# Attention and gated MLP on one core: which engine copies kv wo, the first attention product in four matmuls, and a new hand-searched order

## The chip, the cores and the metric

One core of one Trainium2 chip. Its engines are TensorE (PE), VectorE (DVE), ScalarE (ACT), GpSimd (POOL) and SyncE (SP, which here only issues DMA transfers). Each engine works through its own queue in order and waits on semaphores. The metric is the device time of one execution in microseconds; the figure before is the median of three runs.

## The reference

A block of two parts over x of 2048 x 512 (bfloat16), cut to what is computed:

```
ln(t)  = (t - mean) / sqrt(var + 1e-5)
phi(t) = where(t > 0, t + 1, exp(t)) + 1e-6

q, k, v = ln(x) @ wqkv            # 32 heads of 16
kv  = phi(k)^T v                  # per head, 16 x 16
z   = sum over rows of phi(k)
o   = phi(q) kv / (phi(q) z + 1e-6)
h   = x + o @ wo

zz  = gelu(ln(h) @ w_in)          # 1792 wide
z1, z2 = zz[:, :896], ln(zz[:, 896:])
g   = w_sp @ z2 + b_sp            # w_sp is 2048 x 2048
out = h + (z1 * g) @ w_out
```

## The kernel before

The rows are 16 tiles of 128. Everything stays on the chip; x, the weights and the transposed w_sp are loaded, the output is stored.

**Stages.** Row tiles are normalised and transposed (the first four on PE, the rest by DMA transposes, line 673). k products (lines 745 and 756) are followed by phi: ACT's exponential (714) and relu (720), DVE's minimum (716) and sum (722) or, without relu, maximum (725). In place of k and v, the sum over rows of ln(x)^T phi(k) is built up in four PSUM banks (766). After the last tile it is copied (799, 802), multiplied by wv (811), masked to the heads' blocks (820) and multiplied by wo (827): that gives `mw`, kv wo, four blocks of 128 x 512 in PSUM. Blocks 0 and 2 are copied to SBUF by ACT (834), blocks 1 and 3 by DVE (837). q products (858) and phi run between all this in groups of four tiles; a group's denominators are made by a small matmul (871), ACT takes ln and exp (875, 878), SP spreads the result over the partitions (884), and DVE multiplies phi(q) by it (890).

**The attention product** (903) takes, for each row tile, four matmuls of 512 columns that read the four blocks of `mw` in turn; DVE adds x (916), takes the statistics, POOL the power -0.5 (608, 610), DVE normalises, SP transposes. Then come the right half of w_in (959) with gelu on ACT (966 with sums, 974 without), the left half (1013, gelu 1018), the mix with w_sp (1052; DVE 1058, 1060), and the output product (1072, 1076).

**The order.** `build` records each operation with its engine, a cost, what it reads and writes, and a due time `want`. `Program.schedule` (line 151) walks forward in planned time and puts the operations of every engine in a fixed order: of the operations whose predecessors are already placed, each engine takes the one with the lowest planned start plus half its due time. `waits` (line 264) then writes the semaphore waits. On the chip each engine follows its list in order. The due times are the list `WANT` (line 359), one number for each recorded operation, times `UNIT`. `fillers` (line 1097) puts useless matmuls (575) into PE's planned gaps before the first product of line 766, so that PE's clock stays up; eight more run at the start.

**The SP queue.** SP issues all loads (538), the transposes of x and h tiles (673), the spreads (884), and the 64 transposes of w_sp (1032): `wsp0.0` to `wsp0.15` fill the first quarter of the mix's right side, `wsp1.x` the second, and so on. wq, wv, wo, win and wout are one load each (lines 666 to 670).

Of the kernel before, what the change touches and what calls it, by code (L numbers as in the profile page):

```python
# [10 lines left out]
P = 128  # L11
# [81 lines left out]
class Program:  # L93
# [264 lines left out]
UNIT = 0.1  # L358
WANT = [
# [40 lines left out]
def build(nc, A_x, A_wqkv, A_wo, B_w_in, B_w_sp, B_b_sp, B_w_out, out):  # L400
    _, S, D = A_x.shape
    F = B_w_in.shape[1]
    FH = F // 2
# [21 lines left out]
    UNIT_RES = set()  # L425

# [52 lines left out]
    eps = small([4], FP32)  # L479
    mhalf = small([TPG], FP32)  # L480
# [65 lines left out]
    for p in range(1, NP):  # L546
        load("sp", f"x{2 * p}", x[2 * p:2 * p + 2, :],
             x_dram[2 * p * P:(2 * p + 2) * P, :].rearrange("(n p) d -> p n d", p=P), 2 * P * D * 2, -28 + p)

# [89 lines left out]
    def T1(n):  # L639
        return 5.2 + 1.85 * n  # L640

    rs1, cT = {}, {}
    for grp in LN1:
        rs = small([len(grp)], FP32)
        nm = small([len(grp)], FP32) if any(n in ACT_NORM1 for n in grp) else None
        for n in grp:
            stats(x[n, :], Row(st_x, n), T1(n) - 4, f"st{n}")
            aggr(Row(st_x, n), 6, T1(n) - 4, f"ag{n}")
        lo, hi = grp[0], grp[-1] + 1
        for n in grp:  # L650
            if n in LATE:
                d, m = xc[n].all(), st_x[n, 6:7]
                cT[n] = Tile(XC)
                op("dve", dve_f(512), lambda e, n=n, d=d, m=m: e.tensor_scalar(d.ap(), x[n, :].ap(), m.ap(), None,
                                                                              op0=ALU.subtract),
                   r=[x[n, :], m], w=[d, cT[n]()], want=T1(n) - 3, name=f"xc{n}")
        rstd_act(st_x[lo:hi, 7], rs.all(), T1(lo) - 2.5, f"rs{lo}")
        if nm is not None:
            minus_mean(st_x[lo:hi, 6], rs.all(), nm.all(), T1(lo) - 2.5, f"nm{lo}")
        for i, n in enumerate(grp):  # L660
            rs1[n] = rs[i:i + 1]
            if n in ACT_NORM1:
                normalise_act(xn[n, :], x[n, :], nm[i:i + 1], rs[i:i + 1], T1(n) - 2, f"xn{n}")
            else:
                normalise(xn[n, :], x[n, :], st_x[n, 6:7], rs[i:i + 1], T1(n) - 2 + 4 * (n in LATE), f"xn{n}")
# [3 lines left out]
    load("sp", "win", win.all(), B_w_in.rearrange("(c p) f -> p c f", p=P), D * F * 2, 30.2)  # L669
    load("sp", "wout", wout.all(), B_w_out.rearrange("(c p) f -> p c f", p=P), FH * D * 2, 30.3)  # L670
# [133 lines left out]
    for b in range(2):  # L804
# [26 lines left out]
        for i in range(2):  # L831
            d = mw[2 * b + i, :]
            if i == 0:
                op("act", act_c(512), lambda e, t=t, d=d: e.activation(d.ap(), t(bank(0)).ap(), ACT.Copy), r=[t()], w=[d],
                   want=T0 + 3.5 + b, name=f"mwc{2 * b}")
            else:
                op("dve", dve_c(512), lambda e, t=t, d=d: e.tensor_copy(d.ap(), t(bank(1)).ap()), r=[t()], w=[d],  # L837
                   want=T0 + 3.5 + b, name=f"mwc{2 * b + 1}")
# [54 lines left out]
    hn_t, hn_op = {}, {}  # L893
    for p in range(NP):
        t = Tile(PS, 2)
        for ti in range(2):
# [4 lines left out]
            def mm(e, t=t, ti=ti, l=l, n=n, unit=unit):  # L901
# [5 lines left out]
                return i  # L907
            op("pe", pe_c(*[512] * (4 + unit)), mm, r=[l, mw.all()] + ([x[n, :], ident.all()] if unit else []), w=[t()],
# [12 lines left out]
    for grp in LN2:  # L921
# [8 lines left out]
        for i, n in enumerate(grp):  # L930
            t = hn_t[n] = Tile(HN)
            if n in ACT_NORM2:
                hn_op[n] = normalise_act(t(), x[n, :], nm[i:i + 1], rs[i:i + 1], w0 + 1 + 0.1 * i, f"hn{n}")
            else:
                hn_op[n] = normalise(t(), x[n, :], st_h[n, 6:7], rs[i:i + 1], w0 + 1 + 0.1 * i, f"hn{n}")

# [3 lines left out]
    for p in range(NP):  # L940
# [11 lines left out]
        for n in (2 * p, 2 * p + 1):  # L952
# [12 lines left out]
            if n in ACT_Z:  # L965
                op("act", (act_c(FH)[0] + 0.1, act_c(FH)[1] + 0.1), lambda e, t=t, d=d, n=n: e.activation(  # L966
# [6 lines left out]
            else:  # L973
                op("act", act_c(FH), lambda e, t=t, d=d: e.activation(d.ap(), t(flat).ap()[:, 0:FH], ACT.Gelu_apprx_tanh),
# [52 lines left out]


# [149 lines left out]
```

## Time and profile before

| | |
|---|---|
| runs (us) | 243.06, 242.39, 242.1; median 242.39 |
| profiled execution: device time, span | 242.13 us, 240.4 us |
| TensorE clock granted | 1.0 of full speed, throughout |
| POOL busy | 14.2 us (6%) |
| DMA | 24.18 MB, mean 101 GB/s |
| attention products (903) in the chain that ended last | 5.8% of the span |
| mix products (1052) in that chain | 40.0% of the span |

A row of an instruction view gives start, length, engine, line, operation, tiles and count; brackets give the engine's idle time just before and who ended it. The ends of matmuls are modelled: a matmul's row is longer than its distance to the next one. The chain of waits gives start, length, and the work that held the end up in that stretch. In tables by stretch the columns are the stretch, its length, the busy time and instruction count of PE, PE's weight loads, DVE, ACT and POOL, the granted clock, the DMA engines' mean busy share, and GB/s.

### The profile page before, as it was taken

Reading aid. Unit: us, or ns where it says so; the run is one execution under the profiler, and the core shown is the slowest. Engines: PE = TensorE matmul, PEld = TensorE weight load, DVE = VectorE, ACT = ScalarE, POOL = GpSimd, SP = SyncE. Lnnn points to the kernel's source line nnn. Section 1 sums busy time; section 2 is a strip of 40 time slices with the busy share of each in tenths; the row PEclk is TensorE's granted clock in tenths of the full one; section 3 lists DMA queues with packets and bytes.
Section 4 is the critical chain, followed back from the end, with each engine's and each line's share of the span. In section 5 each row is a group of like instructions: output and inputs, shape, how many; then the busy total and the mean of one; then the engine's idle time right before and its main releaser. Section 6 shows DMA issues by size and latency. Waiting matters only on the chain.

```text
span 240.4 us, 3056 instructions
## 1 busy us (share of the span) xinstructions
PE 235.1 (98%) x1177; PEld 108.6 (45%) x1199; DVE 127.4 (53%) x270; ACT 83.4 (35%) x131; POOL 14.2 (6%) x33
## 2 busy tenths in 40 slices
PE   8999999999999999999999999999999999999996
PEld 2444445444444544444444444444444444444443
DVE  5999756299999983227212333324333433332443
ACT  4898965566065799994211100000000000000000
POOL 3000000001202160213000000000000000000000
PEclk9999999999999999999999999999999999999999
DMA  6986789632632545445444544452200001000022
GB/s 195 292 206 81 206 199 313 225 102 95 173 84 56 88 100 107 91 99 100 99 97 104 83 99 108 93 107 66 87 0 0 25 22 44 0 3 0 0 87 87
DMA packets 61805, 24.18 MB, mean 101 GB/s; under 512 B 52064, under 2 KB 61152, under 8 KB 61792
## 3 DMA queue, kind: packets, MB, share of 16 engines
q1 hardware_dynamic: 61648, 23.97, 41.2%
q8 instruction: 9, 0.15, 0.3%
q10 hardware_dynamic: 144, 0.03, 0.1%
q14 instruction: 4, 0.03, 0.1%
HBM read 7.47 MB, written 2.10 MB: 40 GB/s over the span
## 4 chain that ended last, share of the span: by engine, by line
PE 94%; DVE 3%; ACT 1%; issue 1%
PE ps L1052 40%; PE ps L1072 10%; PE ps L959 10%; PE ps L1013 10%; PE ps L903 6%; PE ps L766 6%; PE ps L756 5%; PE ps L858 4%; PE ps L575 2%; DVE hT L802 1%; DVE k_xn_z L837 1%; DVE xT_pq_z L890 0%; PE ps L684 0%; DVE xT_pq_z L725 0%; PE ps L778 0%
## 5 line engine op out<-in xcount | busy, mean ns | idle before, releaser
L1052 PE MATMUL ps<-wsp,k_xn_z 128*128 128x512 bf16 x328 | 73.6, 379 | 0.4
L1058 DVE TENSOR_TENSOR e<-ps,e 128x512 bf16<-128x512 f32 x28 | 19.4, 691 | 69.2 <-PE ps L1052 69.2
L1052 PEld LDWEIGHTS ps<-wsp,k_xn_z 128*128 128x128 bf16 x336 | 32.9, 98 | 39.7
L1013 PE MATMUL ps<-hT,win 128*128 128x512 bf16 x110 | 26.0, 379 | 0.1
L959 PE MATMUL ps<-win,hT 128*128 128x384 bf16 (+1 forms) x126 | 25.3, 352 | 0.1
L1072 PE MATMUL ps<-wout,xT_pq_z 128*128 128x512 bf16 (+2 forms) x125 | 25.1, 355 | 0.1
L1052 PE MATMUL ps<-wqkv_wsp,k_xn_z 128*128 128x512 bf16 x110 | 24.2, 379 | 0.1
L1018 ACT ACTIVATE xT_pq_z<-ps 128x1024 bf16<-128x1024 f32 x14 | 14.1, 1021 | 25.5 <-PE ps L1013 25.5
L587 DVE BATCH_NORM_STATS2 small<-xh 128x6 f32<-128x512 bf16 x32 | 21.0, 679 | 3.0 <-DMA xh<-in_A_x_dram 2.9
L959 PEld LDWEIGHTS ps<-win,hT 128*128 128x128 bf16 x128 | 12.5, 98 | 12.4
L1072 PEld LDWEIGHTS ps<-wout,xT_pq_z 128*128 128x128 bf16 x126 | 11.8, 98 | 12.7
L1052 PEld LDWEIGHTS ps<-wqkv_wsp,k_xn_z 128*128 128x128 bf16 x112 | 11.0, 98 | 13.2
L1013 PEld LDWEIGHTS ps<-hT,win 128*128 128x128 bf16 x112 | 11.0, 98 | 12.6
L1076 DVE TENSOR_TENSOR e<-ps,xh 128x512 bf16<-128x512 f32 (+2 forms) x18 | 11.3, 632 | 9.7 <-PE ps L1072 9.2
L714 ACT ACTIVATE e<-ps 128x1024 bf16<-128x1024 f32 (+1 forms) x16 | 15.4, 970 | 2.0 <-PE ps L756 1.1
L766 PE MATMUL ps<-k_xn_z 128*128 128x512 bf16 x63 | 15.2, 379 | 0.2 <-issue 0.2
L858 PE MATMUL ps<-xT_pq_z,wqkv_wsp 128*128 128x512 bf16 x61 | 15.0, 379 | 0.1
L903 PE MATMUL ps<-k_xn_z,xT_pq_z 128*128 128x512 bf16 x62 | 14.0, 379 | 0.6 <-DVE k_xn_z L837 0.4
L966 ACT ACTIVATE k_xn_z<-ps 128x896 bf16<-128x896 f32 x12 | 10.9, 909 | 9.2 <-PE ps L959 9.2
L756 PE MATMUL ps<-wqkv_wsp,xT_pq_z 128*128 128x512 bf16 x55 | 13.2, 379 | 0.3 <-ACT xT_pq_z L699 0.2
L1060 DVE TENSOR_TENSOR xT_pq_z<-xT_pq_z,e 128x512 bf16<-128x512 bf16 x28 | 11.9, 425 | 2.2 <-ACT xT_pq_z L1018 1.3
L970 ACT ACTIVATE e<-k_xn_z 128x896 bf16<-128x896 bf16 x12 | 11.4, 949 | 0.3
(75 smaller groups left out, 168.6 us busy)
## 6 DMA issues: line engine op xcount, KB each, us to landing
wsp<-e SPq DMA_DIRECT2D x16, 128.0 KB
out_dram<-e SPq DMA_DIRECT2D x15, 128.0 KB, 1.7
xh<-in_A_x_dram SPq DMA_DIRECT2D x7, 256.0 KB, 3.8
win<-in_B_w_in_dram SPq DMA_DIRECT2D x1, 1792.0 KB, 7.5
wqkv_wsp<-in_A_wqkv_dram SPq DMA_DIRECT2D x3, 512.0 KB, 5.7
wout<-in_B_w_out_dram SPq DMA_DIRECT2D x1, 896.0 KB, 5.3
wsp<-in_B_w_sp_dram SPq DMA_TRANSPOSE x48, 2.7
wqkv_wsp<-in_A_wo_dram SPq DMA_DIRECT2D x1, 512.0 KB, 5.0
```

What stands on the lines that cost most here:

```text
L587: op("dve", (0.577, 0.69), lambda e: e.bn_stats(row[0:6].ap(), src.ap()), r=[src], w=[row[0:6]], want=want, name=name)
L714: first = op("act", act_c(n, ptr=len(pt)), lambda e: e.activation(e_(ev).ap(), src(t), ACT.Exp, scale=sc), r=[t()] + pt, w=[e_()], want=wa ...
L756: i = e.matmul(t(bank(ti)).ap(), lhsT=lhs.ap()[:, c, :], rhs=rhs.ap()[:, c, :], start=(c == 0), stop=(c == KD - 1))
L766: i = e.matmul(HT(bank(j)).ap(), lhsT=xn[n, j * P:(j + 1) * P].ap(), rhs=pk[n, :].ap(), start=(n == 0), stop=(n == NT - 1))
L858: k = e.matmul(t(bank(i)).ap(), lhsT=lhs.ap()[:, c, :], rhs=rhs.ap()[:, c, :], start=(c == 0), stop=(c == KD - 1))
L903: i = e.matmul(t(bank(ti)).ap(), lhsT=l.ap()[:, c, :], rhs=mw[c, :].ap(), start=(c == 0), stop=(c == KD - 1 and not unit))
L959: k = e.matmul(t(bank(i)).ap()[:, 0:b - a], lhsT=l.ap()[:, c, :], rhs=win[c, a:b].ap(), start=(c == 0), stop=(c == KD - 1))
L1013: k = e.matmul(t(bank(i)).ap(), lhsT=l.ap()[:, c, :], rhs=r_.ap()[:, c, :], start=(c == 0), stop=(c == KD - 1))
L1018: op("act", act_c(1024), lambda e: e.activation(d.ap(), t(None if same else flat).ap(), ACT.Gelu_apprx_tanh), r=[t()], w=[d], want=want + ...
L1052: k = e.matmul(t(bank(0)).ap(), lhsT=l.ap()[:, s - a, :], rhs=r_.ap()[:, s - a, :], start=(s == 0), stop=(s == NT - 1))
L1058: op("dve", dve_c(512), lambda e: e.tensor_tensor(gb().ap(), t(bank(0)).ap(), bsp().ap()[:, tg * GW:(tg + 1) * GW], ALU.add), r=[t(), bsp( ...
L1072: k = e.matmul(t(bank(0)).ap()[:, 0:r_.ap().shape[-1]], lhsT=l.ap()[:, fc, :], rhs=r_.ap()[:, fc, :], start=(fc == 0), stop=(fc == KF - 1))
```

## The change

- ACT copies blocks 0, 2 and 3 of `mw`; DVE copies block 1 alone.
- The attention product of row tile 2 (`FIRST_O = 2`) is recorded as four operations of one matmul each, on blocks 2, 0, 1, 3 in this order, each reading its own block.
- The load of win has to come after the normalisation of row tile 15 (`xn_op`); the load of wout is recorded after the left-half products and has to come after the gelu of row tile 8 (`g2_op`).
- `UNIT` is 0.02 in place of 0.1, and all of `WANT` is new. From the output products on, and for the mix products of the last two quarters, the due times are the same as before in microseconds.

```
-UNIT = 0.1
+UNIT = 0.02
 WANT = [
...
+    FIRST_O = 2
...
-    load("sp", "win", win.all(), B_w_in.rearrange("(c p) f -> p c f", p=P), D * F * 2, 30.2)
-    load("sp", "wout", wout.all(), B_w_out.rearrange("(c p) f -> p c f", p=P), FH * D * 2, 30.3)
+    load("sp", "win", win.all(), B_w_in.rearrange("(c p) f -> p c f", p=P), D * F * 2, 30.2, after=[xn_op[NT - 1]])
...
-            if i == 0:
-                op("act", act_c(512), lambda e, t=t, d=d: e.activation(d.ap(), t(bank(0)).ap(), ACT.Copy), r=[t()], w=[d],
-                   want=T0 + 3.5 + b, name=f"mwc{2 * b}")
+            if i == 0 or b == 1:
+                op("act", act_c(512), lambda e, t=t, d=d, i=i: e.activation(d.ap(), t(bank(i)).ap(), ACT.Copy), r=[t()],
+                   w=[d], want=T0 + 3.5 + b, name=f"mwc{2 * b + i}")
             else:
                 op("dve", dve_c(512), lambda e, t=t, d=d: e.tensor_copy(d.ap(), t(bank(1)).ap()), r=[t()], w=[d],
                    want=T0 + 3.5 + b, name=f"mwc{2 * b + 1}")
...
+            if n == FIRST_O:
+                for k, c in enumerate((2, 0, 1, 3)):
+                    op("pe", pe_c(512), lambda e, t=t, ti=ti, l=l, k=k, c=c: e.matmul(
+                        t(bank(ti)).ap(), lhsT=l.ap()[:, c, :], rhs=mw[c, :].ap(), start=(k == 0), stop=(k == KD - 1)),
+                       r=[l, mw[c, :]], w=[t()], want=TO(p) + 0.01 * k, name=f"o{n}.{c}" if k else f"o{n}")
+                continue
...
+    load("sp", "wout", wout.all(), B_w_out.rearrange("(c p) f -> p c f", p=P), FH * D * 2, 300.0, after=[g2_op[8]])
```

The due times (in us) that the prediction speaks of:

| load or transpose | before | after |
|---|---|---|
| wv | 39.6 | 19.4 |
| wo | 39.0 | 58.0 |
| win | 31.8 | 32.1 |
| wout | 24.8 | 88.06 |
| wsp1.0 | 109.7 | 108.24 |
| wsp0.12 | 111.0 | 109.54 |

More of the change, by code (lines that the diff above doesn't have):

```diff
@@ L640, in T1 @@
         return 5.2 + 1.85 * n
-    rs1, cT = {}, {}
+    rs1, cT, xn_op = {}, {}, {}
     for grp in LN1:
@@ L662, in build @@
             if n in ACT_NORM1:
-                normalise_act(xn[n, :], x[n, :], nm[i:i + 1], rs[i:i + 1], T1(n) - 2, f"xn{n}")
+                xn_op[n] = normalise_act(xn[n, :], x[n, :], nm[i:i + 1], rs[i:i + 1], T1(n) - 2, f"xn{n}")
             else:
-                normalise(xn[n, :], x[n, :], st_x[n, 6:7], rs[i:i + 1], T1(n) - 2 + 4 * (n in LATE), f"xn{n}")
+                xn_op[n] = normalise(xn[n, :], x[n, :], st_x[n, 6:7], rs[i:i + 1], T1(n) - 2 + 4 * (n in LATE), f"xn{n}")
     load("sp", "wq", wqkv[:, 0:D], w3[:, :, 0:D], D * D * 2, 27)
@@ L891, in build @@
                r=[d, r_], w=[d], want=wd + 2, name=f"sc{gq}.{h}")
-    hn_t, hn_op = {}, {}
+    hn_t, hn_op, g2_op = {}, {}, {}
     for p in range(NP):
@@ L965, in build @@
             if n in ACT_Z:
-                op("act", (act_c(FH)[0] + 0.1, act_c(FH)[1] + 0.1), lambda e, t=t, d=d, n=n: e.activation(
+                g2_op[n] = op("act", (act_c(FH)[0] + 0.1, act_c(FH)[1] + 0.1), lambda e, t=t, d=d, n=n: e.activation(
                     d.ap(), t(flat).ap()[:, 0:FH], ACT.Gelu_apprx_tanh, accum_out=st_z[n, 14:15].ap()), r=[t()],
@@ L973, in build @@
             else:
-                op("act", act_c(FH), lambda e, t=t, d=d: e.activation(d.ap(), t(flat).ap()[:, 0:FH], ACT.Gelu_apprx_tanh),
+                g2_op[n] = op("act", act_c(FH), lambda e, t=t, d=d: e.activation(d.ap(), t(flat).ap()[:, 0:FH],
+                                                                               ACT.Gelu_apprx_tanh),
                    r=[t()], w=[d], want=TZ(p) + 1.5, after=lnexp, name=f"g2.{n}")
```

74 rows, old and new, of the table WANT are left out of this document.

## The prediction

> **What bounds it now.** I read the busy shares first, then TensorE by stage, then the chain that ended last around the one stage with a hole, then the instructions in that hole, then the DMA queue.
>
> ```profile
> span 240.4 us, 3056 instructions
> PE 235.1 (98%) x1177; PEld 108.6 (45%) x1199; DVE 127.4 (53%) x270; ACT 83.4 (35%) x131; POOL 14.2 (6%) x33
> ```
>
> PE (TensorE) is busy for 235.1 of 240.4 us, and the change removes no matmul. So what can be won is PE's idle time and its filler matmuls, and nothing else. Where that lies (columns: stretch, its length, then busy time and instructions by engine):
>
> ```profile
> 4.80:9.70 4.90, 4.65 (x28) 2.14 (x27) 4.81 (x16) 3.50 (x10) 0.00 (x0) 1.00 1.12 343
> 30.00:40.00 10.00, 9.69 (x104) 4.66 (x104) 5.96 (x10) 6.87 (x8) 0.00 (x0) 1.00 0.99 264
> 48.30:54.24 5.94, 5.47 (x40) 2.76 (x39) 5.93 (x11) 3.91 (x6) 0.00 (x0) 1.00 0.31 97
> 57.50:65.00 7.50, 7.50 (x35) 3.26 (x35) 7.47 (x16) 2.42 (x3) 1.30 (x2) 1.00 0.57 164
> ```
>
> From 57.5 us on PE has no hole to speak of. Between 48.30 and 54.24 it lacks 0.47 us, and there DVE is busy for 5.93 of 5.94. The chain of waits names the same place:
>
> ```profile
> 50.80 0.34 DVE hT L820
> 51.14 0.39 DVE e L716
> 51.52 0.33 DVE hT L820
> 51.85 1.13 DVE xT_pq_z L725
> 52.98 1.21 DVE k_xn_z L837 x2
> 54.19 0.05 issue
> 54.24 2.76 PE ps L903 x12
> 57.00 0.33 PE ps L871 x4
> ```
>
> Instructions there (start, length, engine, line):
>
> ```profile
> 52.23 1.08 ACT L834 ACTIVATE k_xn_z<-ps 128x512 bf16<-128x512 f32 x2 [1.16 <-PE ps L827]
> 52.90 1.28 DVE L837 CAST k_xn_z<-ps 128x512 bf16<-128x512 f32 x2
> 53.41 0.40 PE L871 MATMUL ps<-xT_pq_z,small 128*32 128x512 bf16 x4
> 53.52 1.03 ACT L714 ACTIVATE e<-ps 128x1024 bf16<-128x1024 f32 x1 [0.21 <-PE ps L858]
> 55.15 1.22 DVE L725 SCALAR_TENSOR_TENSOR xT_pq_z<-ps,e 128x1024 bf16<-128x1024 f32 x1
> ```
>
> ScalarE (ACT) has copied its two blocks of the product kv wo by 53.31, while DVE, held by the maximum of L725, ends its two at 54.18. The first attention product (L903) needs all four and starts at 54.24, 0.50 after PE finished the denominator matmuls (53.41 + 0.33 from the chain's other L871 piece = 53.74).
>
> **Third copy to ScalarE, product in four.** ACT's two copies take 0.594 us each and start 0.49 apart, so three run at 52.23, 52.72 and 53.21 and end at 53.81. DVE's one copy starts at 52.98 behind the maximum and takes 0.68: 53.66. The first matmul needs only block 2, the first that ACT copies; the later matmuls follow 0.22 apart (PE's 12 in 2.76 us, less the last one's modelled end). PE is free at 53.74; block 2 is ready at 52.77, and all four at 53.81, ahead of the second matmul at 53.96 whichever block it is. So the hole closes. Gain 0.42 (the idle time that the trace puts before L903) to 0.50 (54.24 - 53.74); I take 0.45. Three more waits on PE: bounded by zero and by the 0.05 of the "issue" piece each, 0 to 0.15; I take 0, since a wait already met shows no gap between neighbouring groups elsewhere in the chain.
>
> The Trainium skill (ScalarE: Activation LUTs, Rules for kernel authors) speaks against this move: simple element work belongs on VectorE, up to about three times faster in bf16. The trace disagrees for this form, a copy from f32 in PSUM: ACT 594 ns, DVE 679 ns. By the rule DVE's two copies would be done by about 53.4 (an estimate, a third of ACT's time each) and there would be no hole to close, so the gain would be 0.
>
> **What stands behind the third copy.** ACT's next is the exponential of L714, at 53.52. It moves to about 53.78, 0.26 later; its followers on DVE are the minimum (0.42) and the maximum of L725, which ended at 56.37, so 56.63 now, 0.3 sooner at best where the freed 0.6 us of DVE helps. The next denominator (L871) ran at 56.93; with PE 0.45 earlier it would be due at 56.48. Wait: 0.15, or 0 if the new order puts another product between. Loss 0 to 0.25; I take 0.1.
>
> **wout moved to the end of the gelu stage.** It leaves the place at 25.16 and now waits for the gelu of tile 8, the last L974 (start 107.94, 0.92 long, so 108.86), now 108.41. Its due time is 88.06 (4403 x 0.02), far under those of the spatial-weight transposes left in SP's queue (wsp1.0 108.24, wsp0.12 109.54). As the planner takes the lowest of start + half the due time, wout goes ahead of both as soon as the gelu is planned. What a copy does to transposes behind it, from the old place (the last column of the issue rows is us to landing):
>
> ```profile
> 25.16 0.58 SPq L538 DMA_DIRECT2D wout<-in_B_w_out_dram  x1
> 25.78 1.24 SPq L1032 DMA_TRANSPOSE wsp<-in_B_w_sp_dram  x1
> wout<-in_B_w_out_dram SPq DMA_DIRECT2D x1, 896.0 KB, 5.3
> wsp<-in_B_w_sp_dram SPq DMA_TRANSPOSE x1, 5.1
> xT_pq_z<-k_xn_z SPq DMA_TRANSPOSE x1, 4.4
> xT_pq_z<-k_xn_z SPq DMA_TRANSPOSE x1, 2.5
> ```
>
> 2.5 us undisturbed (issued 23.84), 5.1 directly behind wout, 4.4 for the next (issued 27.07). The transposes now behind it serve the first whole mix product:
>
> ```profile
> 102.43 10.78 SPq L1032 DMA_TRANSPOSE wsp<-in_B_w_sp_dram  x8
> 115.47 3.45 PE ps L1052 x16
> ```
>
> Today wsp0.12 is the eighth of those eight, issued at 111.94, landed 2.7 later at 114.64: 0.83 us of cover before 115.47. After: wout 108.5, wsp1.0 109.1, wsp0.12 110.4, landed at 114.8; the product is due at 115.02. The cover falls to 0.2. If SP is 0.6 later (its transposes sit 1.3 apart, with a gap of 1.69 once in this stretch), PE waits 0.4, and all behind it on PE; with 5.1 to landing in place of 4.4 it waits 1.1. Loss 0 to 1.1; I take 0.15. wout itself is needed at 165.5 and lands near 114.
>
> **The front's order, wv, wo, win.** wv's due time falls from 39.6 to 19.4, wo's rises to 58.0 but SP takes it whenever nothing lower is ready; both are needed near 50. win waits for the last normalised tile (ACT, about 29) and was issued at 32.33 anyway, landing at 39.8 for a use at 65.2: cost 0, covered by 25 us. The reordered first 48 us can win at most what PE lacks there, about 0.5 of idle time outside the hole, and 1.4 us of fillers between 5.16 and 9.7 (1.06 + 0.38); they can lose one transpose wait, priced below. Most of the order's pieces abut already, so I take 0.
>
> **Sum.** -0.45 + 0.1 + 0.15 = -0.20. The profiled execution took 242.13 (span 240.40, 1.73 around it), 0.26 under the median 242.39. So span 240.2, and 242.2 for the median.
>
> **Rivals.** *A: given back whole.* The wait for wsp0.12 comes in full (1.1), with 0.1 of the denominators' wait: -0.45 + 1.2 = +0.75, 243.1. For it: the cover falls from 0.83 to 0.2. Against: SP may run as early as worked out.
>
> *B, slower: wv in front of the k tiles.* The transpose of x tile 8 was issued at 23.84 and landed 2.5 later at 26.34; the k product of its unit starts at 27.03, so 0.69 of cover. A 512 KB copy issued less than one transpose ahead makes 5.1 of 2.5, so PE stands 2.6 - 0.69 = 1.9 us, in order, nothing to slip past. It decides as soon as the added delay is above 0.69. 242.2 + 1.9 = 244.1. For it: wv's due time now lies right in that stretch, and the due times of tiles 9, 10 and 11 (28.7) are behind it. Against: wout, nearly twice as large, leaves the same stretch, and other k units can be ordered ahead.
>
> *C, faster: the start shrinks.* If the reordered first loads and normalisations close the stretch that two fillers occupy (1.06 us from 5.16), on top of 0.45: 242.39 - 1.5 = 240.9. For it: the order of x4, x6, x8 and wq changes. Against: the first product waits on x0, its statistics and wk, which keep their places.
>
> **Chances.** Forecast (241.6 to 242.6) 0.38, A 0.21, B 0.25, C 0.16. About 0.5%, 1.2 us, is what a measurement of this kernel can tell from no change: faster is below 241.2, slower above 243.6. C gives faster 0.16; B, less its mildest tail, and A's worst give slower 0.25; the rest is 0.59. The range, 240.9 to 244.1, reaches over A and into B and C; it leaves out about 0.1 at each end.
>
> **What would show it.** Step one: three L834-like copies on ACT and no PE idle before the first attention product. Step two: PE's wait before the next L871. Step three: wout issued near 108.5, and a PE wait before the product at 115. B: a PE wait ahead of a k product between 18 and 32 us. C: fewer than the twelve matmuls of L575. A PE stretch after 120 us that is not as dense as before would prove me wrong altogether.

## The result, and the profile after

The changed kernel takes 243.85 us (median of 12 runs, 243.03 to 244.73), the kernel before 242.6 (12 runs, 241.72 to 243.43). The ratio is 1.0055, 95% interval 1.0037 to 1.0073: slower by some 1.3 us, where 0.2 less was forecast. The profiled executions' spans are 242.1 and 240.4 us.

```profile
span 242.1 us, 3076 instructions
PE 235.5 (97%) x1199; PEld 108.0 (45%) x1199; DVE 127.2 (53%) x269; ACT 83.6 (35%) x132; POOL 13.7 (6%) x33
```

PE's work is the same within 0.4 us, so its waits grew. The table by stretch shows where; its columns are those of the table shown for the kernel before. First two stretches of the kernel before, then four of the changed kernel:

```profile
20.00:30.00 10.00, 9.95 (x47) 4.42 (x47) 8.57 (x20) 9.09 (x13) 0.00 (x0) 1.00 0.71 154
65.00:75.00 10.00, 9.95 (x49) 4.77 (x49) 9.60 (x22) 5.12 (x9) 2.21 (x4) 1.00 0.29 79
...
20.00:30.00 10.00, 8.43 (x40) 3.63 (x39) 7.92 (x19) 7.31 (x10) 0.00 (x0) 1.00 0.88 135
48.30:54.24 5.94, 5.94 (x41) 3.14 (x39) 5.23 (x9) 2.89 (x5) 0.00 (x0) 1.00 0.43 139
57.50:65.00 7.50, 7.22 (x36) 2.95 (x35) 6.84 (x12) 2.54 (x3) 0.95 (x2) 1.00 0.44 142
65.00:75.00 10.00, 9.84 (x50) 4.49 (x48) 9.87 (x20) 4.10 (x8) 2.12 (x4) 1.00 0.41 105
```

Two things stand out. Between 20 and 30 us PE now lacks 1.57 us; the same stretch before lacked 0.05. And the hole of 48 to 54 us, which the change was aimed at, is closed, while in the two stretches after 57.5, where PE had lacked 0 and 0.05 us, it now lacks 0.28 and 0.16. PE's own rows say who ended each wait. The first two are of the kernel before (PEld is PE's weight load), the rest of the changed kernel, whose line numbers are 2 to 11 higher (758 is the k product, 768 the sum, 860 the q product, 873 the denominators, 892 DVE's multiplication, 905 the attention product, 912 its first one, in four, 968 the right half of w_in):

```profile
24.43 1.89 PE L756 MATMUL ps<-wqkv_wsp,xT_pq_z 128*128 128x512 bf16 x8
61.73 3.14 PEld L903 LDWEIGHTS ps<-k_xn_z,xT_pq_z 128*128 128x128 bf16 x16 [0.47 <-DVE xT_pq_z L890]
...
23.76 1.03 PE L768 MATMUL ps<-k_xn_z 128*128 128x512 bf16 x4
26.28 1.89 PE L758 MATMUL ps<-wqkv_wsp,xT_pq_z 128*128 128x512 bf16 x8 [1.49 <-DMA xT_pq_z<-k_xn_z]
...
54.99 0.40 PE L873 MATMUL ps<-xT_pq_z,small 128*32 128x512 bf16 x4
55.32 1.04 PE L912 MATMUL ps<-k_xn_z,xT_pq_z 128*128 128x512 bf16 x4
...
63.16 3.63 PE L905 MATMUL ps<-k_xn_z,xT_pq_z 128*128 128x512 bf16 x16 [0.28 <-DVE xT_pq_z L892]
...
68.46 1.90 PE L905 MATMUL ps<-k_xn_z,xT_pq_z 128*128 128x512 bf16 x8 [0.16 <-DVE xT_pq_z L892]
```

A bracket counts from the modelled end of the matmul before. Matmuls of 512 columns start 0.22 us apart but have rows of 0.38, so a wait counted by the starts is 0.16 longer than its bracket.

The k product of tiles 10 and 11 waits 1.49 us for a DMA transpose. The first attention product (L912) follows the denominators (L873) without a gap: 54.99 + 0.33 = 55.32. Then tile 12's product waits for DVE's multiplication by the reciprocals (L892), and so does tile 6's. SP's queue shows what the first of these waits is made of:

```profile
19.48 0.58 SPq L540 DMA_DIRECT2D wqkv_wsp<-in_A_wqkv_dram  x1
20.10 1.19 SPq L675 DMA_TRANSPOSE xT_pq_z<-k_xn_z  x1
21.34 1.26 SPq L675 DMA_TRANSPOSE xT_pq_z<-k_xn_z  x1
```

and the DMA view of the same three issues, in the same order, gives the time from issue to landing in its last column:

```profile
wqkv_wsp<-in_A_wqkv_dram SPq DMA_DIRECT2D x1, 512.0 KB, 5.7
xT_pq_z<-k_xn_z SPq DMA_TRANSPOSE x1, 5.5
xT_pq_z<-k_xn_z SPq DMA_TRANSPOSE x1, 4.8
```

The load at 19.48 is wv. The two transposes behind it, of tiles 11 and 10, land 5.5 and 4.8 us after issue; the second is there at 21.34 + 4.8 = 26.14, and PE starts at 26.28.

The starts of the same operations in both traces give the account:

| operation on PE | before | after | later by | in this step |
|---|---|---|---|---|
| k product of tile 6 | 20.12 | 20.31 | 0.19 | +0.19 |
| k product of tile 10 | 24.43 | 26.28 | 1.85 | +1.66 |
| first product with wv (L811, now L813) | 49.84 | 51.41 | 1.57 | -0.28 |
| first attention product | 54.24 | 55.32 | 1.08 | -0.49 |
| first whole mix product | 115.31 | 117.07 | 1.76 | +0.68 |

The aim was met (-0.49). It was given back (+0.68), and 1.66 came on top before any of it. The first 0.19 is a wait for the transpose of tile 6, which landed 4.0 us after its issue (3.5 in the kernel before); no run tries it by itself.

### The profile page after: what moved, and what is told of

It reads as the page before. It is cut to its first block, busy times and chain, and to the rows that moved or that the text cites. A ratio compares the mean times of both kernels' runs of the same rounds, so it can differ in the third digit from the quotient of the medians.

```text
span 242.1 us, 3076 instructions
## 1 busy us (share of the span) xinstructions
PE 235.5 (97%) x1199; PEld 108.0 (45%) x1199; DVE 127.2 (53%) x269; ACT 83.6 (35%) x132; POOL 13.7 (6%) x33
## 4 chain that ended last, share of the span: by engine, by line
PE 82%; DVE 8%; DMA 4%; ACT 3%; SPq 1%; issue 0%
PE ps L1063 40%; PE ps L1083 10%; PE ps L1023 10%; PE ps L968 9%; PE ps L768 4%; PE ps L860 3%; PE ps L758 3%; DVE small L590 3%; DMA xT_pq_z<-k_xn_z 2%; PE ps L905 1%; DMA wsp<-e 1%; DMA xh<-in_A_x_dram 1%; DVE xh L924 1%; DVE xT_pq_z L892 1%; DVE k_xn_z L617 1%; SPq L886 1%
## 5 line engine op out<-in xcount | busy, mean ns | idle before, releaser
L1069 DVE TENSOR_TENSOR e<-ps,e 128x512 bf16<-128x512 f32 x28 | 19.4, 692 | 69.2 <-PE ps L1063 69.2
L968 PE MATMUL ps<-win,hT 128*128 128x512 bf16 (+1 forms) x128 | 25.8, 352 | 0.0
L968 PEld LDWEIGHTS ps<-win,hT 128*128 128x128 bf16 x128 | 12.4, 98 | 12.8 <-issue 0.3
L758 PE MATMUL ps<-wqkv_wsp,xT_pq_z 128*128 128x512 bf16 x56 | 13.2, 379 | 1.7 <-DMA xT_pq_z<-k_xn_z 1.5
L718 DVE TENSOR_SCALAR e<-e 128x1024 bf16<-128x1024 bf16 (+1 forms) x18 | 7.0, 391 | 9.8 <-ACT e L716 9.7
```

The costliest lines, as they stand in the source:

```text
L758: i = e.matmul(t(bank(ti)).ap(), lhsT=lhs.ap()[:, c, :], rhs=rhs.ap()[:, c, :], start=(c == 0), stop=(c == KD - 1))
L968: k = e.matmul(t(bank(i)).ap()[:, 0:b - a], lhsT=l.ap()[:, c, :], rhs=win[c, a:b].ap(), start=(c == 0), stop=(c == KD - 1))
L1069: op("dve", dve_c(512), lambda e: e.tensor_tensor(gb().ap(), t(bank(0)).ap(), bsp().ap()[:, tg * GW:(tg + 1) * GW], ALU.add), r=[t(), bsp( ...
```

## The experiments

Each changes the finished lists of a kernel, after the planner is done: where one operation stands, which engine has it, or into how many parts it is split. `place(g, engine, a, b)` moves operation a in its engine's list to right behind b; edit lines that are not code tell the change in words. Times are beside runs of the kernel before on the same chip. Line numbers move a little from run to run: 890, 892 and 894 are the same multiplication, 903, 905 and 907 the same product.

### wv back, in the changed kernel

```
+    place(g, "sp", "wv", "wo")
```

> The changed kernel with one load moved: wv goes from ahead of the transposes of x tiles 11 and 10 to behind wo in SP's queue; nothing else moves. Theory Q (the copy in the queue makes the k product of tile 10 wait): PE's 1.49 us wait at 26.28 is gone, that product starts at 24.6 to 24.8, the span falls from 242.1 to 240.4 to 240.7. Theory S (the slower time comes from the third ScalarE copy and what stands behind it): the wait at 26.28 stays or comes back elsewhere, span 241.8 to 242.2.

Measured: span 240.5; 242.21 us against 242.22, ratio 0.9997 (0.9981 to 1.0013).

```profile
24.76 1.89 PE L758 MATMUL ps<-wqkv_wsp,xT_pq_z 128*128 128x512 bf16 x8
...
53.80 1.04 PE L912 MATMUL ps<-k_xn_z,xT_pq_z 128*128 128x512 bf16 x4
...
61.55 3.63 PE L905 MATMUL ps<-k_xn_z,xT_pq_z 128*128 128x512 bf16 x16 [0.18 <-DVE xT_pq_z L892]
```

PE's rows show the three places at issue. The transposes of tiles 11 and 10, issued at 19.33 and 20.64 with no load ahead, landed after

```profile
xT_pq_z<-k_xn_z SPq DMA_TRANSPOSE x1, 4.0
xT_pq_z<-k_xn_z SPq DMA_TRANSPOSE x1, 3.2
```

so wv ahead of them made the landing 1.5 and 1.6 us longer (5.5 and 4.8), and the issue 0.7 later besides. Why they took more than the 2.5 us of others without a load ahead was not followed up.

One load's place is the whole loss. The product of tile 10 starts at 24.76 with no wait, and the kernel is as fast as the one before. It is not faster, though the first attention product still starts with no hole: the wait before tile 12 is still there.

### wv early, in the kernel before

```
+    place(g, "sp", "wv", "tx7")
```

> The kernel before with the same one load moved the other way: wv between the transposes of x tiles 7 and 10. Theory Q: the product of tile 10 (24.43 before) waits until the transposes behind wv have landed, about 20.8 + 4.8 = 25.6 and 0.14 on, so 1.2 us longer: span 241.3 to 241.9. Theory S: nothing, span 240.3 to 240.6.

Measured: span 243.3; ratio 1.0036 (1.0012 to 1.0060).

```profile
26.29 1.89 PE L756 MATMUL ps<-wqkv_wsp,xT_pq_z 128*128 128x512 bf16 x8 [1.61 <-DMA xT_pq_z<-k_xn_z]
...
64.64 3.63 PE L903 MATMUL ps<-k_xn_z,xT_pq_z 128*128 128x512 bf16 x16 [1.31 <-DVE xT_pq_z L890]
```

The same move alone makes the same wait, 1.61 us, in a kernel with nothing else of the change. The profiled execution was the slowest of the twelve (245.02 us, median 242.89): it has 1.31 us more before tile 12, behind a spread that took 4.58 us in the chain of waits, where the changed kernel's took 2.94. Why that landing was so late in this execution was not followed up. The timed runs show 0.9 us on the whole (0.3 to 1.5), less than the 1.2 expected and much less than the profiled one.

### The third copy and the split, in the kernel before

```
+    mwc3: from DVE to ACT, behind mwc0
+    o2: four operations, blocks 2, 0, 1, 3
```

> The kernel before with only the third copy on ScalarE (in the order 2, 0, 3) and the product of tile 2 in four matmuls; every other place in every queue as before. Theory Q with the prediction's sum: the 0.42 us hole before the first attention product closes and the gain stays: span 239.9 to 240.1. Theory S: the exponential, ln and exp behind the third copy start 0.3 us later, so do the four spreads, and the product of tile 12 (61.73 before, just in time) waits: the hole closes but the gain comes back as a wait there, span 240.3 to 240.8.

Measured: span 240.8; ratio 1.0012 (0.9988 to 1.0037).

```profile
53.81 0.40 PE L873 MATMUL ps<-xT_pq_z,small 128*32 128x512 bf16 x4
54.14 1.04 PE L1150 MATMUL ps<-k_xn_z,xT_pq_z 128*128 128x512 bf16 x4
...
60.13 1.90 PE L905 MATMUL ps<-k_xn_z,xT_pq_z 128*128 128x512 bf16 x8 [0.15 <-DVE xT_pq_z L892]
62.19 3.63 PE L905 MATMUL ps<-k_xn_z,xT_pq_z 128*128 128x512 bf16 x16 [0.15 <-DVE xT_pq_z L892]
```

The hole closes here too (54.14 is 53.81 + 0.33), and two waits appear that were not there, for two multiplications of the same line, those of tiles 8 and 9 and of tiles 12 and 13. (In this edit the first of the four matmuls also waits for block 0, which ScalarE has done by 53.71.) This execution started 0.65 us later than the profiled one of before (first k product by L756 at 10.36, not 9.71), so the spans are not to be compared. From that product to the first attention product it is 43.78 us here and 44.53 before: 0.49 of the difference is the hole, and 0.26 a wait for tile 12's transpose that is not met here (more of it under wout below). From the first attention product to the first product of L963 (L959 before) it is 11.51 us here and 10.95 before, 0.56 longer. So what the hole gave is given back whole, with nothing else of the change in place. The runs show no gain.

### Half of wv

In the changed kernel, the first 256 KB of wv in its place, the rest behind wo.

```
+    wv:  wqkv[0:2, 2 * D:3 * D]
+    wvb: wqkv[2:4, 2 * D:3 * D], behind wo
```

> The changed kernel with wv in two loads of 256 KB: the first half in wv's place, the second behind wo. If the transposes wait for the bytes of the copy ahead of them, PE's wait before the product of tile 10 falls to 0.5 to 0.9 us, span 241.1 to 241.5. If any copy ahead costs the same, whatever its size, the wait stays 1.3 to 1.6 us.

Measured: span 240.7, wait 0.20 us; ratio 1.0002 (0.9977 to 1.0028). The transposes behind the half landed in 4.5 and 3.7 us, 1.0 and 1.1 sooner than behind the whole. Against the run with no load ahead (4.0 and 3.2) the half adds 0.5 us to each, the whole 1.5 and 1.6. So the delay grows with the bytes, and the wait fell further than I expected: I had scaled the wait, but it is the delay less a fixed cover, 21.07 + 3.7 = 24.77 against a product due at 20.23 + 4.32 = 24.55 (its distance from tile 6's product in the run with wv back).

### Two places later, and the two transposes exchanged

```
+    place(g, "sp", "wv", "tx10")        # one run
+    place(g, "sp", "tx11", "tx10")      # another, wv left ahead of both
```

> The changed kernel with wv two places later only, behind the transposes of tiles 11 and 10 and still ahead of those of 8 and 9. If it is the place ahead of the transpose that PE needs next: the 1.49 us wait goes, span 240.4 to 240.8. If a copy anywhere among the transposes costs it: a wait of 1 us or more before the product of tile 8 (27.2), span 241.5 or more.

Measured: no wait before tile 10, but 0.74 us before tile 8, span 241.5 (one execution). The two answers had left this middle out: moving the copy moves the wait to the next transpose behind it, whose cover is larger. There tiles 8 and 9 landed in 4.2 and 4.0 us.

> The changed kernel with the transposes of tiles 11 and 10 exchanged, wv still ahead of both. PE needs tile 10 first. If the landing behind the copy is what PE waits for: tile 10 lands at 20.10 + 5.5 = 25.6 instead of 26.15 and the wait falls by 0.5 to 0.6 us, to about 0.95. If the order of the two is the cause rather than wv: the wait goes altogether.

Measured: the wait is 1.32 us, span 242.1 (one execution). Tile 10, now first, landed 6.0 us after its issue at 20.22, so at 26.22, no sooner than as the second (26.14). But wv itself took 6.2 us here, not 5.7, which takes up the half microsecond that I had worked out, so one execution doesn't say what the order is worth. It does say that the order is not the cause: with it mended, the wait is still there.

### wv from ScalarE's queue

```
+    wv: issued by ACT, behind xn9; no longer in SP's list
```

> The changed kernel with wv issued by ScalarE at the same time (behind the normalisation of tile 9, 19.6), not by SP; SP's transposes keep their order, now with no copy among them. If a transpose only suffers from a copy ahead of it in the same queue: the wait before the product of tile 10 goes, landing 2.5 to 3.2, span 240.4 to 241.0 (ScalarE 0.6 later). If the two share what carries them, whoever issues: the transposes still take over 4 us, and a wait of 0.5 to 1.5 us stays, span 241.2 to 242.3.

Measured: span 245.3 (one execution), worse than every other. ACT issued wv at 18.38, 1.1 us sooner than SP had, so it met other transposes, and the run does not compare the two queues at one place. SP issued the transposes of tiles 7, 11 and 10 at 17.75, 19.21 and 20.44. They landed after

```profile
xT_pq_z<-k_xn_z SPq DMA_TRANSPOSE x1, 6.8
xT_pq_z<-k_xn_z SPq DMA_TRANSPOSE x1, 5.7
xT_pq_z<-k_xn_z SPq DMA_TRANSPOSE x1, 4.7
```

and it was tile 7, the next one needed, that was late, though it was issued 0.6 us ahead of wv. PE's rows:

```profile
24.56 1.89 PE L758 MATMUL ps<-wqkv_wsp,xT_pq_z 128*128 128x512 bf16 x4 [3.19 <-DMA xT_pq_z<-k_xn_z]
28.62 1.03 PE L768 MATMUL ps<-k_xn_z 128*128 128x512 bf16 x4
```

and two rows of this run's table by stretch, in which the third column from the right is the granted clock:

```profile
18.00:24.00 6.00, 3.37 (x16) 1.24 (x14) 5.78 (x15) 3.48 (x5) 0.00 (x0) 1.00 1.23 169
24.00:30.00 6.00, 5.39 (x18) 2.23 (x20) 0.61 (x3) 3.12 (x4) 0.00 (x0) 0.72 0.32 66
```

Here another queue did not help: SP's transposes were late with no load among them in SP's list, so the copy and the transposes share something, whoever issues them. The Trainium skill (DMA: Bandwidth & Descriptors, Issuing engines are not separate DMA queues) says that transfers from any engine run on the same 16 DMA engines and interleave; these rows agree, with 6.8, 5.7 and 4.7 us where the same three transposes took 2.5, 4.0 and 3.2 in the run with wv behind wo.

### What eats the closed hole

Two runs, both with wv behind wo, so that this loss alone is left.

```
+    sp3.1, sp3.3: from SP to ACT, behind rd3
```

> The changed kernel with wv behind wo, and in addition two of the four spreads of group 3's reciprocals issued by ScalarE right behind the exp that makes them, in place of SP. Theory Q+S (with wv out of the way, the waits before the products of tiles 12 and 6 are what eats the closed hole, and they come from the chain third copy, exponential, ln, exp, four spreads in a row on SP): the spreads are all out 1.2 us sooner, the 0.53 us in which DVE waited for them and PE's 0.18 us wait before tile 12 go, span 240.0 to 240.3 against 240.5 of the kernel with wv alone moved back. If the spreads' own transfer time is what counts, not their issue: both waits stay, span 240.5.

Measured: span 240.5; ratio 0.9994 (0.9968 to 1.0019). The last of the four spreads was issued 0.7 us sooner, not 1.2 (ACT issued its two at 55.74 and 57.22, SP's last had been at 57.93), and 0.24 of that is only that this execution ran ahead (first attention product at 53.56, not 53.80). It gained nothing: DVE waited 0.69 us for the spreads and started at 60.72 where it had started at 60.80, 3.5 us after the last issue instead of 2.9, and PE's wait before tile 12 was 0.34 by its bracket, not 0.18. That is the second answer, both waits stay. What made the landing take longer the runs do not show.

```
+    mwc3: from ACT back to DVE, behind mwc1; o2 stays split
```

> The changed kernel with wv behind wo and the third copy given back to DVE, behind its own; the product of tile 2 stays in four matmuls, the last of which reads that block. If the split alone closes the hole: the first attention product still starts right behind the denominators and the span is 240.3 to 240.5, since ScalarE's chain runs 0.5 us sooner. If DVE is the bound of the stretch: the hole moves to the next denominators, whose phi comes 0.6 us later from DVE, span 240.8 to 241.1.

Measured: span 240.4; 242.08 against 242.35 us, ratio 0.9989 (0.9963 to 1.0015).

```profile
53.80 1.04 PE L914 MATMUL ps<-k_xn_z,xT_pq_z 128*128 128x512 bf16 x4
54.68 1.89 PE L907 MATMUL ps<-k_xn_z,xT_pq_z 128*128 128x512 bf16 x8
57.09 0.40 PE L875 MATMUL ps<-xT_pq_z,small 128*32 128x512 bf16 x4 [0.52 <-DVE xT_pq_z L727]
57.42 7.94 PE L907 MATMUL ps<-k_xn_z,xT_pq_z 128*128 128x512 bf16 x36
```

The place of the wait is the second answer's, the span the first's. The hole moves to the next denominators, whose phi DVE ends later: 0.52 us. But now the 36 matmuls behind them run in one piece, with no wait before tile 12 (nor before tile 6). That is not because the multiplication comes sooner: PE itself gets there later, since these denominators run at 57.09 and not at 56.55. DVE's multiplication for tile 12, in the kernel before, with wv back, with two spreads on ACT, and with the copy back on DVE:

```profile
60.99 0.68 DVE L890 TENSOR_TENSOR xT_pq_z<-xT_pq_z,wsp 128x1024 bf16<-128x1024 bf16 x1
60.80 0.69 DVE L892 TENSOR_TENSOR xT_pq_z<-xT_pq_z,wsp 128x1024 bf16<-128x1024 bf16 x1 [0.53 <-DMA wsp<-e]
60.72 0.69 DVE L892 TENSOR_TENSOR xT_pq_z<-xT_pq_z,wsp 128x1024 bf16<-128x1024 bf16 x1 [0.69 <-DMA wsp<-e]
60.73 0.68 DVE L894 TENSOR_TENSOR xT_pq_z<-xT_pq_z,wsp 128x1024 bf16<-128x1024 bf16 x1
```

It starts within 0.3 us in all four, while the first attention product starts at 54.24, 53.80, 53.56 and 53.80. A product that reaches it sooner waits. Whichever engine makes the copy, the same half microsecond is lost, in one of two places.

No version run was measurably faster than the kernel before.

## Why the prediction was wrong

**The step that failed** is "the front's order": "Most of the order's pieces abut already, so I take 0". I had read that wv's due time fell into the stretch of the k tiles' transposes and had the price of it from wout's row (5.1 us for 2.5), made a rival of it with 0.25, and put nothing of it into the sum. It cost 1.66 us between tiles 6 and 10. The measured time lies inside the range, 240.9 to 244.1, and goes the other way than the sum. Rival B was the outcome: its mechanism, its place (a PE wait ahead of a k product between 18 and 32 us), and nearly its time, 244.1 against 243.85. It named tile 8; the wait came at tile 10, whose transpose stood second behind wv. That the number came so near is in part luck: B had the landing 2.6 us longer with 0.69 of cover. Against the run with wv back, tile 10's transpose landed 2.3 us later (26.14, not 23.84), of which 1.6 is a longer landing and 0.7 a later issue, and there it had 0.9 of cover (23.84 to 24.76). And 2.5 us was not what every transpose takes with no load ahead: in the kernel before, those of tiles 11 and 9 took 4.2 and 3.5, which the prediction leaves out. What I said against B, that wout leaves the same stretch, is no argument: wout stood behind the eight transposes of tiles 4 to 11, wv ahead of four of them.

**The hole.** Right: forecast 0.45, the account has 0.49 in this step. By the Trainium skill's rule on simple element work (ScalarE: Activation LUTs, Rules for kernel authors) there would have been nothing to close. The page gives its factor for bf16; these copies read f32 from PSUM, where DVE takes 0.68 us and ACT 0.59, and the rule had no hold here.

**What stands behind the third copy.** Forecast +0.1, at the denominators. They waited 0.05 more than before. I followed ScalarE's chain to the next denominators and stopped; it goes on to the ln and exp of group 3, four spreads, DVE's multiplication and the product of tile 12. In the kernel before, that product was just in time: its weight load, at 61.73, waited 0.47 for the multiplication, and its first matmul started 0.14 later than 0.22 behind the one before it. So whatever closed earlier opened there. Measured by the starts: 0.44 before tile 12, which is 0.30 more than before, and 0.32 before tile 6 (its product starts at 68.46, the eight matmuls of L968 ahead of it start at 66.63 and need 1.51). Tile 6's product stands behind eight matmuls of L968 in the new list and behind sixteen of L959 in the old one, so that wait belongs to the new order as well as to the copy. The run with the copy back on DVE agrees: these waits go, and another of about their size comes.

**wout.** Forecast +0.15, range to 1.1. There was no wait at the first whole mix product. wout was issued behind wsp0.12, not ahead of it, since the transposes had moved up further than I worked out: the last of them, wsp0.12, was issued at 110.50, before the gelu of tile 8 ended at 110.62.

```profile
99.80 11.96 SPq L1043 DMA_TRANSPOSE wsp<-in_B_w_sp_dram  x9
111.81 1.77 SPq L540 DMA_DIRECT2D wout<-in_B_w_out_dram  x1
```

Its leaving the front is no gain that these runs show. In the kernel before, the k product of tile 12 started 1.12 us after the L766 row ahead of it (31.62 and 30.50; 0.86 when nothing waits), for a transpose that landed at 27.07 + 4.4 = 31.47, behind wout. That 0.26 is gone in the changed kernel, and it is the -0.28 of the table. But there PE comes to this product at 33.19, so a landing at 31.47 would have been in time too: 0.28 of wv's 1.66 went into a wait that was there already. In the run with the third copy and the split, wout stands in its old place, PE came 0.39 later, and this wait was gone as well. What wout's leaving is worth once wv is back was not tried by itself.

**A and C.** The gain was given back whole, as in A, but not where A had it. The start did not shrink (C): the first k product by PE's L758 starts at 9.68, before at 9.71.

## What to carry to other kernels

A load with no hurry is not free where it stands: price it by what is behind it in time, and take the transposes' landing behind a copy, not the copy's own deadline. In the one run that tried it, another queue was no way round it. And when a hole on a saturated engine is closed, follow PE's next products until one needs something that does not come sooner; if that one was just in time before, the gain ends there.

## What the runs showed that I had not expected

- Transposes behind a copy in SP's queue landed one after another once the copy was through. Behind wv: copy at 19.48 + 5.7 = 25.18, transposes at 25.60 and 26.14; with the two exchanged: 25.75, then 26.22 and 26.76 (21.46 + 5.3); behind half of wv: 23.80 (19.20 + 4.6), then 24.32 and 24.77. So some 0.5 us apart in these three runs. With wv two places later the second came about 1 us behind the first, and with wv on ACT's queue the copy was through at 18.38 + 4.4 = 22.78 but the first transpose landed at 24.5. With no load ahead, about 2.5 us from issue is the least that they took.
- PE's 3.19 us wait in the run with wv on ScalarE's queue cost more than itself: the granted clock between 24 and 30 us was 0.72 of full speed, and the first four matmuls behind the wait took 1.89 us where four take 1.03. The Trainium skill (TensorE: Matmul & The Clock Gate, What's actually happening) puts the return to half clock at an idle window of about 3.4 us. This run agrees: counted by the starts the wait is 3.19 + 0.16 = 3.35 us. The waits of 1.5 us in the other runs left the clock at 1.0.
- Issued from ScalarE while SP was issuing too, the first of two spreads took 1.44 us to issue (55.74 to 57.18) where SP needs 0.61.
- Starts differ between executions: the first k product by L756 or L758 stood at 9.60 to 10.36 us in the profiled ones, as much as most of the effects here.
